# Fused attention and two MLPs on one Trainium2 core: batch 7 and the tails are projected together, by seven half-size products

## The chip, the cores and the metric

The kernel runs on one core of a Trainium2 chip. The metric is device time in microseconds (us) of one execution, from the inputs in the chip's memory to the output there. Engines are named as in the profile: PE (TensorE, matmul), PEld (its weight loads), DVE (VectorE), ACT (ScalarE), POOL (GpSimd), SP (the queue from which nearly all transfers are issued).

## What is computed

```python
def _attn_ref(q, k, v, p):            # q, k, v: (8, 8, 576, 64), p: (8, 8, 32, 64)
    p_packed = sm_attn(p, k, v)       # 32 packed rows per head attend to 576 rows
    out = sm_attn(q, p_packed, p_packed)

def _moe_ref(x, w_in, w_out):         # x: (4608, 512), w_in: (512, 2048), w_out: (2048, 512)
    h = x @ w_in
    g = h * (1.0 / (1.0 + np.exp(-h)))
    return g @ w_out

def _moe2_ref(x, w_in, w_out):        # same shapes
    h = x @ w_in
    g = h * np.clip(h + 3.0, 0.0, 6.0) / 6.0
    return g @ w_out
```

The output is `_moe2(_moe(attention))` over 8 x 576 = 4608 rows.

## The kernel before

A product in single precision is made of three TensorE products of rounded halves: a value is split into a high part (an ACT cast) and a low part (a DVE subtraction), and high x high, high x low and low x high are summed. One such TensorE product has 512 columns and is called a matmul below.

**First phase.** The 4608 rows are worked on as 9 blocks of 512: block j = 0 to 7 holds the first 512 rows of batch j, block 8 the 8 x 64 rows left over, the tails. `block(j)` runs over the 16 chunks f of the hidden dimension. `hidden(j, f)` makes the hidden chunk: 6 matmuls in blocks 0 to 7 (weights `fused`, which `fuse` has made from the packed values and w_in of the first MLP, four chunks at a time; operand `a2`, the attention weights) and 12 in the tails (weights `win`, operand `xh`, `xl`). Then ACT applies Silu in place in the PSUM bank (L891), `split_g` makes the high part on ACT (L898) and the low part on DVE (L899), and two chunks later `projects` multiplies them by w_out: 12 matmuls (L906 to L908) into four accumulators. So PE alternates between hidden chunks and projections. At a block's end ACT and DVE copy the accumulators out, with a write of stride 4 that sorts the rows (L974), and SP stores them to `x1d`.

Beside this stream the attention of batch j + 1 runs, as steps that `attention` lists with a place in the block and waits in units of PE time, and that `Plan` places between matmuls. Its q, k and v come through a ring of 6 tiles called `nat`: the next tile is asked for when one has been used, and SP's transfer waits until DVE has transposed what lay in the buffer. The four v tiles (L348) are used by the packed product (L490, L493). The hidden banks and the attention's banks come from the same four PSUM banks `ps_h`; `fuse` takes two of them.

Half of w_out (even f) stays in the tiles `wr`; odd f is loaded again for each block (`next_out`, L234) into three tiles `wo`.

**Preparation.** The second MLP needs its weights as seven sums of blocks each, so that a product of 2 x 2 blocks takes seven products instead of eight. Class `Prep` makes these from block 1 on, in 32 units, one after the other: load, two ACT steps (L157, L163), two DVE steps, a POOL sum (L297), four DVE sums (L300 to L303), two ACT casts (L305, L306), two POOL subtractions (L308, L309) and three stores. A call of `nxt` between the matmuls runs one step; 9 steps make a unit.

**Second phase.** Class `Second` takes the 4608 rows as five pairs of operands. `Second.project` is its w_out part: 28 steps (7 products x 4 pairs of chunks, order `ORDER_P`) of 12 matmuls, with `sums` (DVE), `split` (ACT cast, DVE subtraction of 128 x 1024) three steps ahead, and weights `ws` by `load_w`.

Of the kernel before, what the change touches and what calls it, by code (L numbers as in the profile page):

```python
# [9 lines left out]
I32 = mybir.dt.int32  # L10
# [8 lines left out]
def tile_pack_attention_two_mlps(ctx: ExitStack, tc, q, k, v, p, w_in1, w_out1, w_in2, w_out2, out):  # L19
# [205 lines left out]
    want_out = [(j, f) for j in range(1, NBLK) for f in range(1, NF, 2)]  # L225
    projected = [-1, -1]

    def next_out():

        now, projected[1] = projected[1], -1 if kept else projected[0]  # L230
        while want_out and now >= NF - 2 and (want_out[0][0] * NF + want_out[0][1]) // 2 <= (now + 1) // 2 - 1 + WO:
            j, f = want_out.pop(0)
            t = half_w(f)
            nc.sync.dma_start(out=f32(t), in_=w1o[f].rearrange("n p f -> p n f"))  # L234
            have_out[j, f] = t
# [4 lines left out]
    w2 = {kind: [dram.tile([S7, P, DM], F32, name=f"w2{kind}{f}", tag=f"w2{kind}{f}") for f in range(HF)] for kind in ("in", "out")}  # L240

    class Prep:


        def __init__(self, pool, w_in, w_out_):
            self.pool = pool
            self.src = {"in": lambda f: win_src(w_in, f), "out": lambda f: wout_src(w_out_, f)}
            self.units = [(kind, f, h) for kind in ("in", "out") for f in range(HF) for h in range(2)]
# [25 lines left out]
        def all(self):  # L274
            self.load(0)
            for _ in range(6):
                yield
            for u, (kind, f, h) in enumerate(self.units):
                key = "p", u
                c = self.pool.tile([P, 8, P], F32, tag="c8", name="c8")  # L280
                hi = self.pool.tile([P, S7, P], F32, tag="hi7", name="hi7", bufs=2)
                conv_begin(key, self.room)
                yield
                yield
                conv_bits(key)
# [12 lines left out]
                yield

                nc.vector.tensor_add(out=c[:, 4], in0=c[:, 2], in1=c[:, 3])  # L300
                nc.vector.tensor_sub(out=c[:, 6], in0=c[:, 0], in1=c[:, 2])
                nc.vector.tensor_sub(out=c[:, 5], in0=c[:, 4], in1=c[:, 0])
                nc.vector.tensor_sub(out=c[:, 7], in0=c[:, 1], in1=c[:, 5])  # L303
                yield
                nc.scalar.copy(out=hi[:, 0:2].bitcast(F32R), in_=c[:, 0:2])  # L305
                nc.scalar.copy(out=hi[:, 2:7].bitcast(F32R), in_=c[:, 3:8])  # L306
                yield
                nc.gpsimd.tensor_sub(out=c[:, 0:2].bitcast(F32R), in0=c[:, 0:2], in1=hi[:, 0:2])  # L308
                nc.gpsimd.tensor_sub(out=c[:, 3:8].bitcast(F32R), in0=c[:, 3:8], in1=hi[:, 2:7])  # L309
                yield  # L310
                yield
                to = w2[kind][f].rearrange("s p f -> p s f")
                nc.sync.dma_start(out=to[:, :, h * P:(h + 1) * P], in_=hi)
                nc.sync.dma_start(out=to[:, 0:2, (2 + h) * P:(3 + h) * P], in_=c[:, 0:2])
                nc.sync.dma_start(out=to[:, 2:7, (2 + h) * P:(3 + h) * P], in_=c[:, 3:8])
# [486 lines left out]
    def attention(b):  # L802
# [18 lines left out]
        add("s", 0.17, 6, lambda: step_s(b), ("kp", 7), (last, 7), bank=9, count=3)  # L821
# [827 lines left out]
```

## Time and profile before

| | us |
|---|---|
| median of 3 runs | 1473.22 (1472.13 to 1473.37) |
| profiled execution, its own time | 1473.38 |
| its span, first to last instruction | 1471.6 |
| PE busy in the span | 1446.9 (98%) |
| DVE, ACT, POOL busy | 1007.9, 725.5, 179.9 |
| moved by transfers | 316.58 MB, 215 GB/s over the span |

Blocks 2 to 6 take some 79 us each, from about 218 to 616 us of the span. Block 7 is the stretch from 616 to 685 us, the tails follow until 774 us, and the rest is the second phase. A busy PE means only that matmuls follow each other; how fast they follow is read from the start times.

### The profile page before, as it was taken

The page shows a single profiled execution, that of the slowest core. Times are in us where ns is not written, and L with a number is a line of the kernel's source. Part 1 is how long each engine was busy: PE and PEld are TensorE (multiplying, and loading weights), DVE is VectorE, ACT ScalarE, POOL GpSimd, SP SyncE. Part 2 cuts the span into 40 slices and gives each one's busy share as a digit, 9 for nine tenths or more (in the row PEclk, how much of TensorE's full clock was granted, in tenths as well). Part 3 has the DMA queues.
Part 4 walks back from the last instruction along what each step waited for, and adds up shares of the span by engine and source line. Part 5 has one row for each costly group of instructions (what it writes and reads, how often), then busy time and mean ns, then how long its engine had stood idle before and what let it go on. Part 6 is the DMA issues. An engine that isn't in the chain of part 4 may idle for free.

```text
span 1471.6 us, 21942 instructions
## 1 busy us (share of the span) xinstructions
PE 1446.9 (98%) x8002; PEld 1178.6 (80%) x8002; DVE 1007.9 (68%) x1555; ACT 725.5 (49%) x1107; POOL 179.9 (12%) x133
## 2 busy tenths in 40 slices
PE   6999999999999999999999999999999999999998
PEld 4767677777777777778888888888888889999998
DVE  5877465566555565545745779776977687788777
ACT  4885455555555555556633344333434353444443
POOL 1440021111112121232320000000000000000000
PEclk9899999999999999999999999999999999999999
DMA  9874868767675866489945575678567866998887
GB/s 289 256 216 131 227 195 214 181 173 181 175 189 163 182 178 174 129 244 254 261 157 194 192 249 195 200 233 260 193 193 224 253 202 218 296 307 252 274 275 224
DMA packets 391051, 316.58 MB, mean 215 GB/s; under 512 B 185120, under 2 KB 288032, under 8 KB 390432
## 3 DMA queue, kind: packets, MB, share of 16 engines
q1 hardware_dynamic: 389048, 314.72, 72.6%
q8 instruction: 64, 1.05, 0.3%
q10 hardware_dynamic: 1896, 0.46, 0.2%
q14 instruction: 43, 0.35, 0.1%
HBM read 257.43 MB, written 57.67 MB: 214 GB/s over the span
## 4 chain that ended last, share of the span: by engine, by line
PE 91%; ACT 4%; DVE 3%; DMA 1%; issue 1%; POOL 0%; SPq 0%; ACTq 0%; POOLq 0%; DVEq 0%
PE acc L906 8%; PE acc L908 8%; PE acc L907 8%; PE b L1172 8%; PE b L1174 8%; PE b L1173 8%; PE b L1267 8%; PE b L1270 8%; PE b L1269 8%; PE hps L879 5%; PE hps L881 5%; PE hps L880 5%; PE abank L426 3%; DMA nat<-in_v_dram 1%; PE abank L490 1%
## 5 line engine op out<-in xcount | busy, mean ns | idle before, releaser
L899 DVE TENSOR_TENSOR gl<-hps,gh 128x512 fp32r<-128x512 f32 x144 | 99.2, 689 | 192.2 <-ACT gh L898 191.8
L1172 PE MATMUL b<-xc,ws 128*128 128x512 f32 (+1 forms) x560 | 205.9, 368 | 0.7 <-ACT x L974 0.7
L1269 PE MATMUL b<-ro,ws 128*128 128x512 f32 (+2 forms) x564 | 206.4, 366 | 0.0
L1270 PE MATMUL b<-ro,ws 128*128 128x512 f32 (+2 forms) x564 | 206.4, 366 | 0.0
L1174 PE MATMUL b<-xc,ws 128*128 128x512 f32 (+1 forms) x560 | 205.8, 367 | 0.0
L1173 PE MATMUL b<-xc,ws 128*128 128x512 f32 (+1 forms) x560 | 205.7, 367 | 0.0
L1215 DVE TENSOR_TENSOR ro<-g,ro 128x1024 fp32r<-128x1024 f32 (+1 forms) x140 | 161.3, 1157 | 42.2 <-ACT ro L1210 41.8
L1210 ACT CAST ro<-g 128x1024 fp32r<-128x1024 f32 (+1 forms) x140 | 131.8, 966 | 94.2 <-DVE g L1203 34.5
L891 ACT ACTIVATE hps<-hps 128x512 f32<-128x512 f32 x144 | 83.9, 583 | 149.9 <-PE hps L881 149.5
L1267 PE MATMUL b<-ro,ws 128*128 128x512 f32 (+2 forms) x564 | 139.0, 367 | 0.3
L906 PE MATMUL acc<-gh,wr 128*128 128x512 f32 x288 | 115.9, 403 | 2.3 <-ACT gh L898 2.3
L1172 PEld LDWEIGHTS b<-xc,ws 128*128 128x128 f32 x560 | 105.2, 188 | 14.2 <-ACT x L974 1.1
L1269 PEld LDWEIGHTS b<-ro,ws 128*128 128x128 f32 x564 | 105.9, 188 | 13.2
L1270 PEld LDWEIGHTS b<-ro,ws 128*128 128x128 f32 x564 | 106.0, 188 | 13.0
L1174 PEld LDWEIGHTS b<-xc,ws 128*128 128x128 f32 x560 | 105.2, 188 | 13.1
L1173 PEld LDWEIGHTS b<-xc,ws 128*128 128x128 f32 x560 | 105.2, 188 | 13.1
L1267 PEld LDWEIGHTS b<-ro,ws 128*128 128x128 f32 x564 | 102.9, 188 | 15.0 <-DVE ro L1215 2.2
L906 PE MATMUL acc<-gh,wo 128*128 128x512 f32 x288 | 113.8, 395 | 0.0
L907 PE MATMUL acc<-gl,wr 128*128 128x512 f32 x288 | 113.4, 394 | 0.2 <-DVE gl L899 0.2
L908 PE MATMUL acc<-gh,wr 128*128 128x512 f32 x288 | 113.3, 393 | 0.0
L908 PE MATMUL acc<-gh,wo 128*128 128x512 f32 x288 | 112.3, 390 | 0.0
L907 PE MATMUL acc<-gl,wo 128*128 128x512 f32 x288 | 112.3, 390 | 0.0
(176 smaller groups left out, 2634.5 us busy)
## 6 DMA issues: line engine op xcount, KB each, us to landing
ws<-w2in SPq DMA_DIRECT2D x280, 256.0 KB
ws<-w2out SPq DMA_DIRECT2D x280, 256.0 KB
wo<-w1o SPq DMA_DIRECT2D x64, 512.0 KB
x1d<-x SPq DMA_DIRECT2D x18, 512.0 KB
raw<-in_moe_w_in_dram SPq DMA_DIRECT2D x16, 512.0 KB
raw<-in_moe_w_out_dram SPq DMA_DIRECT2D x16, 512.0 KB
praw<-in_moe_w_in_dram SPq DMA_DIRECT2D x32, 256.0 KB
praw<-in_moe_w_out_dram SPq DMA_DIRECT2D x32, 256.0 KB
```

The source lines that it names most:

```text
L899: nc.vector.tensor_sub(out=gl, in0=g, in1=f32(gh))
L906: mm(acc[e], lhsT=w[:, 0, s], rhs=gh, start=first, stop=False)
L907: mm(acc[e], lhsT=w[:, 0, s], rhs=gl, start=False, stop=False)
L908: mm(acc[e], lhsT=w[:, 1, s], rhs=gh, start=False, stop=last)
L1172: mm(ps, lhsT=wh, rhs=xs[k][:, 0, c], start=first, stop=False, skip_group_check=True)
L1173: mm(ps, lhsT=wh, rhs=xs[k][:, 1, c], start=False, stop=False, skip_group_check=True)
L1174: mm(ps, lhsT=wl, rhs=xs[k][:, 0, c], start=False, stop=last, skip_group_check=True)
L1210: nc.scalar.copy(out=t[:, 0], in_=v)
L1215: nc.vector.tensor_sub(out=t[:, 1], in0=self.operand(s), in1=f32(t[:, 0]))
L1267: mm(to, lhsT=wh, rhs=x, start=False, stop=last, skip_group_check=True)
L1269: mm(to, lhsT=wh, rhs=x, start=first, stop=False, skip_group_check=True)
L1270: mm(to, lhsT=wl, rhs=x, start=False, stop=False, skip_group_check=True)
```

## The change

Three things are changed.

1. **Batch 7 and the tails as one pair.** Their hidden chunks are computed first, all 16 of batch 7 and then all 16 of the tails. Silu is no longer written in place: ACT writes it from the bank to SBUF tiles `gated`, for batch 7 with the stride of 4 that the block's end had before. Then the new `project_first` multiplies both by w_out as seven products of half size, 28 steps of 12 matmuls, in the way of `Second.project`, and takes over that function's early work for the second phase (`x_steps(0)`).
2. **Preparation.** For this, eight more units ("one") make the seven sums of the first w_out, with 1 KB rows, from the `wr`, `wo` and new `stay` tiles. Units overlap: a unit starts every 10 steps and lasts up to 33. The 40 units run through blocks 1 to 6, batch 7 and 13 of the 16 chunks of the tails; `nxt` runs 1.15 to 1.35 steps per call in 46 calls per block (before: one step in 32 of these calls).
3. **Waits and reloads.** Four of the eight odd w_out chunks stay in SBUF (`STAY`), so four are loaded again per block. Some waits of the attention steps from batch 2 on are shorter or longer by a few units, and all of them from block 1 on are scaled by 1.10.

```diff
-    want_out = [(j, f) for j in range(1, NBLK) for f in range(1, NF, 2)]
+    STAY, SWAP = ((1, 9, 3, 11), (5, 13, 7, 15)), 3
+    stay = {}
+    want_out = [(j, f) for j in range(1, B - 1) for f in range(1, NF, 2)]
...
+    PERIOD, OFFSETS, ONES, ROWS = 10, (3, 13, 16, 17, 18, 21, 23, 25, 29, 31), (0, 6, 4, 12, 8, 13, 29, 28), (9, 33, 20)
...
+                stages = zip(OFFSETS, (self.load, self.begin_unit, self.bits, self.add, self.sums, self.high, self.low, *self.stores(u)))
+                if self.units[u][0] == "one":
+                    stages = zip((*ROWS, *OFFSETS[3:9]), (*self.rows_one(u), self.add_one, self.sums_one, self.high_one, self.low_one, *self.stores_one(u)))
+                for off, fn in stages:
+                    todo.setdefault(PERIOD * u + off, []).append((-off, lambda fn=fn, u=u: fn(u)))
...
+        def add_one(self, u):
+            c = self.c[u] = self.pool.tile([P, 4, 2 * P], F32, tag="c8", name="c1", bufs=2)
+            a, b = (f32(t) for t in self.halves(u))
+            cut = slice(0, 2 * P), slice(2 * P, 4 * P)
+            nc.gpsimd.tensor_add(out=c[:, 1:3], in0=a[:, 0].rearrange("p (r f) -> p r f", r=2), in1=a[:, 1].rearrange("p (r f) -> p r f", r=2))
+            nc.gpsimd.tensor_add(out=c[:, 3], in0=b[:, 0, cut[0]], in1=b[:, 1, cut[0]])
+            nc.gpsimd.tensor_add(out=c[:, 0], in0=b[:, 0, cut[1]], in1=b[:, 1, cut[1]])
...
+        def high_one(self, u):
+            hi = self.hi[u] = self.pool.tile([P, 4, 2 * P], F32, tag="hi7", name="hi1", bufs=2)
+            nc.scalar.copy(out=hi.bitcast(F32R), in_=self.c[u])
+
+        def low_one(self, u):
+            nc.gpsimd.tensor_sub(out=self.c[u].bitcast(F32R), in0=self.c[u], in1=self.hi[u])
...
+        if j >= B - 1:
+            to, src = gated[(f // HF, j - B + 1), f % HF // 2][:, f % 2], ps
+            if j < B:
+                to, src = to.rearrange("p (t i) -> p i t", i=NI), src.rearrange("p (i t) -> p i t", i=NI)
+            nc.scalar.activation(out=to, in_=src, func=AF.Silu)
+            return None
         nc.scalar.activation(out=ps, in_=ps, func=AF.Silu)
...
-            plan.give(11)
+            plan.give(11 if j == 0 else 10)
...
+        def project_first(self):
...
+            for s in range(FD * S7):
+                k, fd = ORDER_P[s // FD], s % FD
+                w, ro = self.weights(), self.ro.pop(s)
+                acc = {1: X, 2: X, 6: Y, 7: Y, 4: Y, 5: Z, 3: Z}[k]
...
+                for lo in range(2):
+                    for f in range(2):
+                        for i in range(2):
+                            wh, wl = (w[:, f, a + i * P:a + (i + 1) * P] for a in (0, 2 * P))
+                            first, last = k in (1, 6, 5) and fd == f == 0, k in (2, 4, 3) and fd == FD - 1 and f == 1
+                            if lo:
+                                mm(acc[i], lhsT=wh, rhs=ro[:, 1, f], start=False, stop=last, skip_group_check=True)
+                            else:
+                                mm(acc[i], lhsT=wh, rhs=ro[:, 0, f], start=first, stop=False, skip_group_check=True)
+                                mm(acc[i], lhsT=wl, rhs=ro[:, 0, f], start=False, stop=False, skip_group_check=True)
+                self.load_w()
...
+                self.sums(s + RO)
+                self.split(s + RO - 1)
+                if s < 2 * FD or s // FD % 2 == 0:
+                    next(prep, None)
...
+    PACE, PACE_LAST, ROOM_AT, X_AT, XS_AT, WIN_AT = (1.25, 1.25, 1.25, 1.35, 1.25, 1.15), (0.9, 0.85), 13, 1, 6, (5, 12, 15)
...
+    for f in range(NF):
...
+        hidden(B - 1, f, nothing, last_work)
+        if f == 2:
+            left()
+        if f % GF == 1 and f // GF + 1 < NG:
+            fuse(B - 1, f // GF + 1)
+        if f == X_AT:
+            load_x()
+        if f in WIN_AT:
+            for g in range(2):
+                win_load(WIN_AT.index(f) * 2 + g)
+        if 0 <= f - XS_AT < KC:
+            split_x(f - XS_AT)
+        if f >= NF - 3:
+            win_split(f - NF + 3)
+    first_right.close()
+    mlp2 = Second()
...
+        hidden(B, f, nothing, last_work if f < ROOM_AT else lambda f, full: None)
...
+    mlp2.project_first()
```

PE, in batch 7, right behind the eight L426 or L488 products that make the second group of hidden weights (the numbers tell tiles apart: `hps` is a hidden bank). Before, a hidden chunk (L879 to L881) is followed by a projection (L906 to L908):

```order
L879 MATMUL hps_6351<-a2h_6113,fused_6154 128x512
L880 MATMUL hps_6351<-a2l_6132,fused_6154 128x512
L881 MATMUL hps_6351<-a2h_6113,fused_6155 128x512
L879 MATMUL hps_6351<-a2h_6223,fused_6157 128x512
L880 MATMUL hps_6351<-a2l_6225,fused_6157 128x512
L881 MATMUL hps_6351<-a2h_6223,fused_6158 128x512
L906 MATMUL acc0_6257<-gh_6289,wo_6198 128x512
L907 MATMUL acc0_6257<-gl_6290,wo_6198 128x512
L908 MATMUL acc0_6257<-gh_6289,wo_6198 128x512
L906 MATMUL acc1_6258<-gh_6289,wo_6198 128x512
L907 MATMUL acc1_6258<-gl_6290,wo_6198 128x512
L908 MATMUL acc1_6258<-gh_6289,wo_6198 128x512
```

The same place now:

```order
L941 MATMUL hps_6394<-a2h_6204,fused_6253 128x512
L942 MATMUL hps_6394<-a2l_6216,fused_6253 128x512
L943 MATMUL hps_6394<-a2h_6204,fused_6254 128x512
L941 MATMUL hps_6394<-a2h_6311,fused_6256 128x512
L942 MATMUL hps_6394<-a2l_6313,fused_6256 128x512
L943 MATMUL hps_6394<-a2h_6311,fused_6257 128x512
L941 MATMUL hps_6409<-a2h_6204,fused_6253 128x512
L942 MATMUL hps_6409<-a2l_6216,fused_6253 128x512
L943 MATMUL hps_6409<-a2h_6204,fused_6254 128x512
L941 MATMUL hps_6409<-a2h_6311,fused_6256 128x512
L942 MATMUL hps_6409<-a2l_6313,fused_6256 128x512
L943 MATMUL hps_6409<-a2h_6311,fused_6257 128x512
```

The projections have moved behind all hidden chunks, so a hidden chunk follows the last one after 6 matmuls instead of 18.

ACT, in the same part of batch 7 (`c8`, `hi7`, `pr`, `praw` are preparation's tiles, `abank` the bank of the hidden weights). Before, a Silu in the bank and a high part per chunk:

```order
L891 ACTIVATE hps_6383<-hps_6383 128x512
L898 CAST gh_6391<-hps_6383 128x512
L157 ACTIVATE pr_6406<-praw_6323 128x512
L163 ACTIVATE praw_6323<-praw_6323 128x512
L891 ACTIVATE hps_6417<-hps_6417 128x512
L898 CAST gh_6427<-hps_6417 128x512
L891 ACTIVATE hps_6451<-hps_6451 128x512
L898 CAST gh_6459<-hps_6451 128x512
L305 CAST hi7_6405<-c8_6404 128x256
L306 CAST hi7_6405<-c8_6404 128x640
L620 CAST fused_6478<-abank_6468 128x512
L620 CAST fused_6481<-abank_6469 128x512
```

Now the Silu writes a gated tile `g` with a stride (4x128), and splits of the tails' operand (`xx`) stand between:

```order
L960 ACTIVATE g04_6421<-hps_6422 128x4x128
L157 ACTIVATE pr_6436<-praw_6306 128x512
L163 ACTIVATE praw_6306<-praw_6306 128x512
L960 ACTIVATE g04_6421<-hps_6430 128x4x128
L682 CAST fused_6456<-abank_6446 128x512
L682 CAST fused_6459<-abank_6447 128x512
L960 ACTIVATE g06_6470<-hps_6471 128x4x128
L1057 CAST xx0_6385<-xx0_6385 128x512
L960 ACTIVATE g06_6470<-hps_6484 128x4x128
L1057 CAST xx1_6387<-xx1_6387 128x512
L960 ACTIVATE g08_6500<-hps_6501 128x4x128
L1057 CAST xx2_6389<-xx2_6389 128x512
```

The high parts are gone from here; since a chunk now takes a third of the matmuls, what is left stands closer together in PE's time.

SP, in block 2, around the loads of the four v tiles (`nat<-in_v_dram`) that the packed product of the next batch needs. Before:

```order
L348 DMA nat_2360<-in_v_dram 128x2x256
L333 DMA pn_2381<-in_p_dram 128x1x64 x2
L339 DMA kt_2384<-in_k_dram 64x8x64
L348 DMA nat_2416<-in_v_dram 128x2x256
L348 DMA nat_2481<-in_v_dram 128x2x256
L234 DMA wo_2497<-w1o7_122 128x2x512
L348 DMA nat_2505<-in_v_dram 128x2x256
L313 DMA w2in1_128<-hi7_2304 128x7x128
```

The same place now:

```order
L410 DMA nat_2347<-in_v_dram 128x2x256
L395 DMA pn_2372<-in_p_dram 128x1x64 x2
L401 DMA kt_2375<-in_k_dram 64x8x64
L334 DMA w2one4_131<-hi1_2317 128x4x256
L410 DMA nat_2406<-in_v_dram 128x2x256
L334 DMA w2one4_131<-c1_2291 128x4x256
L329 DMA w2one2_129<-wr2_705 256x1x256
L410 DMA nat_2472<-in_v_dram 128x2x256
L243 DMA wo_2491<-w1o7_122 128x2x512
L410 DMA nat_2498<-in_v_dram 128x2x256
```

Two stores of 0.5 MB (L334) and one of 0.25 MB (L329) of a "one" unit have come in ahead of the last v tile.

## Rows read from the trace of the kernel before

**Rows 1.** The page, parts 1 and 2: an engine's busy time; PE's granted clock
```profile
PE 1446.9 (98%) x8002; PEld 1178.6 (80%) x8002; DVE 1007.9 (68%) x1555; ACT 725.5 (49%) x1107; POOL 179.9 (12%) x133
...
PEclk9899999999999999999999999999999999999999
```

**Rows 2.** Waits of PE: who waited <- for whom: us, times, longest
```profile
PE abank L490 <- DMA nat<-in_v_dram: 1.8, 1, 1.8
...
PE b L1172 <- ACT x L974: 0.7, 1, 0.7
```

**Rows 3.** Windows: us, busy (instructions) per engine, clock, DMA share, GB/s
```profile
218.00:616.00 398.00, 397.10 (x2529) 293.79 (x2528) 235.25 (x459) 216.49 (x360) 67.44 (x57) 1.00 0.67 175
616.00:685.00 69.00, 69.00 (x337) 54.38 (x336) 30.78 (x61) 40.04 (x71) 21.69 (x18) 1.00 0.84 230
```

**Rows 4.** Timeline of PE in block 7: start us, us, engine, line, operation
```profile
642.98 0.39 PE L879 MATMUL hps<-a2h,fused 128*128 128x512 f32 x1
...
647.06 0.39 PE L879 MATMUL hps<-a2h,fused 128*128 128x512 f32 x1
...
657.04 0.39 PE L908 MATMUL acc<-gh,wr 128*128 128x512 f32 x1
...
658.37 0.50 PE L906 MATMUL acc<-gh,wr 128*128 128x512 f32 x1
```

**Rows 5.** Groups of ACT in block 7: line, operation, count | busy us, mean ns
```profile
L891 ACT ACTIVATE hps<-hps 128x512 f32<-128x512 f32 x16 | 9.3, 582 | 20.5 <-PE hps L881 20.5
L306 ACT CAST hi<-c 128x640 fp32r<-128x640 f32 x6 | 4.4, 729 | 4.1 <-DVE c L303 4.1
L157 ACT ACTIVATE pr<-praw 128x512 f32<-128x512 f32 x6 | 4.1, 677 | 0.0
...
L620 ACT CAST fused<-abank 128x512 fp32r<-128x512 f32 x6 | 3.2, 591 | 1.6 <-PE abank L426 1.6
L305 ACT CAST hi<-c 128x256 fp32r<-128x256 f32 x6 | 2.5, 409 | 0.0
...
L974 ACT COPY x<-acc 128x512 f32<-128x512 f32 x2 | 2.1, 1060 | 3.0 <-PE acc L908 3.0
L222 ACT CAST win<-win 128x512 fp32r<-128x512 f32 x3 | 1.7, 617 | 0.0
```

**Rows 6.** Timeline of ACT in the tails: two starts, and the last copy, without stride
```profile
689.94 0.59 ACT L898 CAST gh<-hps 128x512 fp32r<-128x512 f32 x1
...
692.04 0.58 ACT L891 ACTIVATE hps<-hps 128x512 f32<-128x512 f32 x1
...
773.64 0.58 ACT L974 COPY x<-acc 128x512 f32<-128x512 f32 x1 [0.77 <-PE acc L908]
```

**Rows 7.** Timeline of PE in block 1, around the packed product
```profile
167.32 0.31 PE L490 MATMUL abank<-nat,T 128*32 128x64 f32 x6
169.48 0.63 PE L490 MATMUL abank<-nat,T 128*32 128x64 f32 x26 [1.84 <-DMA nat<-in_v_dram]
...
171.49 0.80 PE L906 MATMUL acc<-gh,wr 128*128 128x512 f32 x1
...
174.10 0.39 PE L879 MATMUL hps<-a2h,fused 128*128 128x512 f32 x1
```

**Rows 8.** The same product on PE in block 3
```profile
330.22 0.65 PE L490 MATMUL abank<-nat,T 128*32 128x64 f32 x32
...
331.88 0.50 PE L906 MATMUL acc<-gh,wr 128*128 128x512 f32 x1
```

**Rows 9.** Window of 10 us in block 2, before its packed product
```profile
235.00:245.00 10.00, 9.93 (x64) 7.26 (x48) 5.28 (x11) 6.30 (x11) 2.26 (x2) 1.00 1.00 280
```

**Rows 10.** Timeline in block 4: a POOL sum of preparation and a DVE step of attention
```profile
352.32 1.57 POOL L309 TENSOR_TENSOR c<-c,hi 128x640 fp32r<-128x640 f32 x1
...
352.73 1.85 DVE L531 TENSOR_TENSOR soft<-soft,s2m 128x640 f32<-128x640 f32 x1
```

**Rows 11.** All of that DVE line: count, min/median/max ns, first to last start
```profile
L531 DVE TENSOR_TENSOR soft<-soft,s2m x16: 691/824/1850, 25.0 to 589.8; 128x512 f32<-128x512 f32 x8, 128x640 f32<-128x640 f32 x8
```

More of the change, by code (lines that the diff above doesn't have):

```diff
@@ L247, in __init__ @@
             self.src = {"in": lambda f: win_src(w_in, f), "out": lambda f: wout_src(w_out_, f)}
-            self.units = [(kind, f, h) for kind in ("in", "out") for f in range(HF) for h in range(2)]
+            rest = [(kind, f, h) for kind in ("in", "out") for f in range(HF) for h in range(2)]
+            ones = dict(zip(ONES, (0, 2, 4, 6, 1, 3, 5, 7)))
+            self.units = [("one", ones[u], 0) if u in ones else rest.pop(0) for u in range(5 * HF)]
+            self.c, self.hi = {}, {}
             self.steps = self.all()
@@ new lines, in all, with halves @@
+            for n in range(max(todo) + 1):
+                for _, fn in sorted(todo.get(n, []), key=lambda x: x[0]):
+                    fn()
+                yield
+        def halves(self, u):
+            f = self.units[u][1]
+            return [made["out", f + n] if f % 2 == 0 else stay[f + n] for n in (0, HF)]
+        def add_one(self, u):
[5 more added lines that the diff above has]
+            nc.gpsimd.tensor_add(out=c[:, 0], in0=b[:, 0, cut[1]], in1=b[:, 1, cut[1]])
@@ new lines, in begin_unit, with bits, add @@
+        def begin_unit(self, u):
+            conv_begin(("p", u), self.room)
+        def bits(self, u):
+            conv_bits(("p", u))
+        def add(self, u):
+            kind, f, h = self.units[u]
+            x, r = raws.pop(("p", u))
+            c = self.c[u] = self.pool.tile([P, 8, P], F32, tag="c8", name="c8", bufs=2)
+            a = c[:, 0:4].bitcast(I32)
+            if kind == "in":
+                a = a.rearrange("p n f -> p (n f)")
+            else:
+                x, r = (t.rearrange("p (b r f) -> p b r f", b=8, r=2) for t in (x, r))
+                a = a.rearrange("p (r n) (b f) -> p (n b) r f", n=2, b=4)
+            nc.gpsimd.tensor_add(out=a, in0=x, in1=r)
@@ L820, in attention @@
             last = f"k{c}"
-        add("s", 0.17, 6, lambda: step_s(b), ("kp", 7), (last, 7), bank=9, count=3)
+        add("s", 0.17, 6, lambda: step_s(b), ("kp", (7 if first else 5)), (last, (7 if first else 5)), bank=(9 if first else 10), count=3)
         steps[-1][4].append((("ut", b - 1), 0))
@@ L1025, in all_chunks @@
         def all_chunks(self):
-            chunks = []
+            chunks = [[w2["one"][2 * fd + i][ROW[k]] for i in range(2)] for k in ORDER_P for fd in range(FD)]
             for n in range(NPAIR):
@@ L1088, in x_steps @@
                 yield
-        def begin_step(self):
-            if next(self.begin, "end") == "end" and self.loaded < WS:
-                self.load_w()
         def bank(self):
@@ L1607, in tile_pack_attention_two_mlps, with last_work @@
             feed.end()
-        if j == B:
-            prep.end()
-        plan.slow = 1
-    for _ in mlp2.begin:
-        pass
+        plan.slow = 1.10
+    def last_work(f, full):
+        share[0] += PACE_LAST[part_[0]]
+        while share[0] >= 1:
+            share[0] -= 1
+            prep.step()
+    part_ = [0]
+    nothing = lambda: None
+    for f in range(NF):
+        if f % 2 == 0:
+            if f < NF // 2:
+                gated[(0, 0), f // 2] = wts.tile([P, 2, T], F32, tag=f"wr{f}", name=f"g0{f}")
+            else:
+                if f % 4 == 0:
+                    two = wts.tile([P, 2, 2, T], F32, tag=f"wr{f}", name=f"g0{f}")
+                gated[(1, 0), f % HF // 2] = two[:, f % 4 // 2]
+        hidden(B - 1, f, nothing, last_work)
[14 more added lines that the diff above has]
+    mlp2 = Second()
+    part_[0] = 1
+    for f in range(NF):
+        if f % 2 == 0:
+            tag, n = [("wo", WO), ("g", LAG), ("x1", 2)][(f // 2 > 2) + (f // 2 > 5)]
+            gated[(f // HF, 1), f % HF // 2] = gp.tile([P, 2, T], F32, tag=tag, name=f"g1{f}", bufs=n)
+        if f == ROOM_AT:
+            prep.end()
+            prep_room.close()
+            mlp2.enter()
+        hidden(B, f, nothing, last_work if f < ROOM_AT else lambda f, full: None)
+        if f % 2 and f < HF:
+            mlp2.t1(f // 2)
+        if f >= NF - 2:
+            mlp2.split(f - NF + 2)
+    mlp2.project_first()
     first_left.close()
```

196 lines of the change are left out of this document (114 added, 82 removed).

## The prediction

> **What bounds the kernel now.** I read the page's busy shares first, then the waits of PE, then the start times of PE, and last what ACT, DVE and POOL do in the stretches that the change touches. PE is busy for 1446.9 of 1471.6 us at a granted clock that stands at full level from the third slice on [rows 1]. Of its waits two matter here, 1.8 us for a v tile in block 1 and 0.7 us at the change of phase [rows 2]; in blocks 2 to 7 it waits for next to nothing (397.10 busy of 398.00, and 69.00 of 69.00) [rows 3]. The chunk that starts at 642.98 and the next one, at 647.06, are 18 matmuls apart: 4.08 us, so one matmul per 0.2267 us [rows 4]. (A row's own 0.39 us is its modelled length, not its pace.) PE is the bound, so the time moves by the matmuls taken away, less each new wait of PE. ACT and DVE have room on the average (235 and 294 of 398 us) [rows 3], and what counts is whether they have it at each place.
>
> **The change part by part.** The counts of instructions, read from the order of both kernels, differ on PE by 48 matmuls of 128x512 and nothing else: w_out of batch 7 and the tails took 2 x 16 x 12 = 384, now 28 x 12 = 336. At 0.2267 us [rows 4] that is **-10.88 us**. It lies on PE's own path whole, since the granted clock is full there [rows 1].
>
> The Trainium skill, "TensorE: Matmul & The Clock Gate", section "Back-to-back issue gap", gives about 131 ns as the sustained spacing of 512-column matmuls; by it the 48 would be worth 6.3 us and the median would come out 4.6 us above my forecast. The trace says otherwise for this kernel's operands, 226.7 ns, and that is what I use.
>
> *Batch 7's hidden chunks.* Before, ACT had 18 matmuls of PE time per chunk, now it has 6: 96 x 0.2267 plus three makings of hidden weights. Such a making costs PE about 1.2 us (658.37 - 657.04, less part of the slot that is there anyway) [rows 4]; together 25.4 us. In that time ACT has to do 16 Silus, and these now write with a stride. No row shows a strided Silu. The bounds are the Silu in place, 582 ns [rows 5], and the strided copy at a block's end, 1060 ns [rows 5], where the copy without a stride takes 0.58 [rows 6]. The write has the same stride as that copy, so I take 1.06: 17.0 us. Beside them stand, by the order, 6 casts of hidden weights (0.591), 3 pairs of high parts (0.409 + 0.729), 2 pairs of L157 and L163 (0.677 for the one, the other taken alike), 4 casts of the tails' operand and 2 of its weights (0.617, one shape) [rows 5]: 3.5 + 3.4 + 2.7 + 3.7 = 13.3 us. One strided copy of block 6, 1.06, falls in too. ACT has 31.4 us of durations for 25.4 us of PE. But ACT's neighbours overlap: from 689.94 to 692.04 four operations with durations of 2.35 us start within 2.10 us [rows 5, 6]. By that factor, 0.89, ACT needs 28.1 us, an overshoot of 2.7 us; without it, 6.0. PE is held only when no hidden bank is free. Of four banks the making of weights takes two, and of the other two one is being filled, so ACT may lag by one chunk, 6 x 0.2267 = 1.4 us. Left is **+1.3 us** (bounds: 0, with the Silu at 0.58 or a lag of two chunks, and 6.0). The tails' chunks have 12 matmuls each and Silus without stride, so ACT catches up there and nothing else is held.
>
> *The projection.* Its 28 steps have the form of the second phase's `project`, which sums, splits and loads in the same way, three steps ahead, and is not among PE's waits [rows 2]; so they cost their matmuls and nothing more. If that cover is gone, a step of 2.7 us (12 x 0.2267) is the most that one late operand costs. The 0.7 us wait at the change of phase [rows 2] stood behind the last strided copies; the new early work `x_steps(0)` runs inside the projection as before inside the tails, so I leave it as it is (bounds: 0.7 gained, 1.2 lost for one step's first operand).
>
> *Preparation and transfers.* The eight new units store three rows of 0.25 MB and two tiles of 0.5 MB each, some 14 MB; 32 reloads of 0.5 MB fall away, so the sum is about even. Per block it is not: about 7.2 units instead of 4 run in blocks 1 to 6, some 1.4 MB each, less four reloads: 2.4 MB more in 79 us, which lifts 175 GB/s [rows 3] to about 205. Block 7 ran at 230 GB/s and a share of 0.84 with no wait of PE [rows 3]. SP's queue is the delicate place: two stores and a row of a "one" unit now stand ahead of v tiles that the packed product needs, and SP serves in order. Already now the 10 us before that product in block 2 run at a share of 1.00 and 280 GB/s [rows 9]. What a late v tile costs is seen in block 1: from the product's first matmul at 167.32 to the next projection at 171.49 it takes 4.17 us, of which 1.84 is the wait, against 330.22 to 331.88, 1.66 us, in block 3; and the six matmuls after it take 2.61 us instead of 6 x 0.2267 = 1.36 [rows 7, 8]. That is 2.5 + 1.2 = **3.7 us per late tile**. The bytes from the block's x1d store to the last v tile, added up along SP's order, are 4.3 MB in block 1 before (late), 2.8 to 4.2 in blocks 2 to 6 (not late), and 3.7 to 4.6 now, with the packed product three matmuls later than before. So the blocks come closer to the edge, but few beyond it. I take **+1.0 us**: a short wait in one or two blocks (bounds: -3.7, if block 1 is on time, and five more events, 18).
>
> *DVE and POOL.* The preparation's POOL sums and subtractions run about twice as often per block. One DVE step took 1.85 us while a POOL subtraction of 1.57 us ran beside it [rows 10]; the same line has a median of 0.824 us and a minimum of 0.691 [rows 11]. So a collision can cost DVE 1.0 us. The attention's steps are placed with room between them (7 to 15 matmuls, 1.6 to 3.4 us), and these are scaled up by 1.10. I take **+0.5 us** (bounds: 0, and 1.0 us in each of six blocks).
>
> Sum: 1473.38 - 10.88 + 1.3 + 1.0 + 0.5 = 1465.3 us. That is against the profiled execution; the median lies 0.16 us lower, so 1465.1.
>
> **The rivals.**
>
> *Nothing new waits.* Banks absorb ACT's lag and every v tile is in time: 1473.2 - 10.9 = 1462.3; with block 1's wait gone too, 1458.6. For it: 69.00 of 69.00 busy at 0.84 [rows 3]. Against: one window at 1.00 [rows 9].
>
> *ACT sets batch 7 in full.* The durations add up as they stand and the makings of weights leave no slack: 1462.3 + 6.0 + 1.5 = 1469.8. For it: the strided copy's 1060 ns [rows 5]. Against: the overlap in [rows 6].
>
> *DVE stands behind POOL in every block.* A collision of 1.0 us falls on the softmax's chain in each of six blocks and the room does not cover it: 1462.3 + 1.3 + 1.0 + 6.2 = 1470.8, about no change. The trace has one such row and fifteen others that are mostly short [rows 11]. The Trainium skill, "GPSIMD Engine Reference", section "1. Specifications", says that POOL shares its SBUF interfaces with VectorE and contends with DVE instructions that have two SBUF inputs; it speaks against more work on POOL, and the stretched row with two such inputs agrees with it [rows 10].
>
> *Late v tiles, slower than before.* The stores on SP's queue push the last v tile of several blocks behind its product, 3.7 us each. After the 10.9 gained and the 1.8 of the other terms some 9 us are left: two and a half events eat the gain, and from four on it is slower: 1462.3 + 1.8 + 14.8 = 1478.9. For it: block 1's event with 4.3 MB ahead [rows 7]. Against: block 3 on time [rows 8] with 4.2 MB ahead.
>
> **How the numbers follow.** Forecast 1465.1, chance 0.56. Nothing new waits: 0.18. ACT in full: 0.08. DVE behind POOL: 0.07. Late v tiles: 0.11. A measurement of this kernel tells about 0.2% from no change: 1470.3 and 1476.2 are the bounds. Faster takes the forecast, the clean case and half of ACT in full, 0.78; same takes the rest of that, DVE behind POOL and a little of the late tiles, 0.12; slower is the rest of these, 0.10. The range runs from just under the clean case, 1461.5, to just over DVE behind POOL, 1472; outside lie the late tiles (0.11) and the clean case with block 1's wait gone (about 0.05).
>
> **What would show it.** PE should have 48 matmuls less, in the stretch of the projection. In batch 7, waits of PE at a hidden bank for ACT's Silu (L960), 1 to 2 us together, with Silus of about 1060 ns; Silus near 600 ns and no wait would mean the clean case. In blocks 1 to 6, waits of the packed product (L552) for v tiles (L410): one short one or two is my sum, one per block the slow rival. DVE steps of the attention above 1.5 us beside POOL in each block, with PE waiting for DVE, would be the third rival. The forecast is wrong if PE's wait in the projection for `ro` or the weights is more than 2 us, or if the granted clock falls in a stretch behind such a wait, of which no row here tells the price except the six slow matmuls in block 1 [rows 7].

## The result

The changed kernel takes 1460.34 us (median of 4 runs, 1459.04 to 1460.55), the kernel before 1473.3 us beside it: a ratio of 0.9915, 95% interval 0.9903 to 0.9927. That is 13.0 us less, where 8.1 us were forecast, and the time lies 1.2 us below the range.

The page of the changed kernel, parts 1 and 2, against [rows 1]:

```profile
PE 1435.6 (98%) x7954; PEld 1167.9 (80%) x7954; DVE 1055.5 (72%) x1603; ACT 748.1 (51%) x1113; POOL 224.4 (15%) x166
...
PEclk8899999999999999999999999999999999999999
```

PE has 11.3 us less to do, in 48 matmuls less; DVE, ACT and POOL have 48, 23 and 45 us more. The waits of PE, against [rows 2] (who waited <- for whom: us, times, longest):

```profile
PE abank L537 <- DVE gg L970: 1.8, 2, 0.9
...
PE b L1396 <- DVE ro L1344: 0.4, 1, 0.4
```

The wait for a v tile is gone, and so is the one at the change of phase. A wait on DVE has come, once in block 0 (there it stood before too) and once in block 4. The 0.4 us on `ro` is not in the new projection but near the end of the second phase:

```profile
1414.35 0.96 PE L1396 MATMUL b<-ro,ws 128*128 128x384 f32 x4 [0.39 <-DVE ro L1344]
```

Where the time went is read by stage: the start of each block's first hidden product in PE's timeline, in the profiled executions. The last column is the whole span.

| us | to block 1 | block 1 | blocks 2 to 6 | batch 7 to second phase | second phase | span |
|---|---|---|---|---|---|---|
| before | 138.4 | 82.6 | 396.4 | 156.9 | 697.3 | 1471.6 |
| after | 138.5 | 78.9 | 397.0 | 146.1 | 698.2 | 1458.7 |
| difference | +0.1 | -3.6 | +0.6 | -10.8 | +0.9 | -12.9 |

So 10.8 us come from the projection, as was worked out, and 3.6 us from block 1, where the forecast had no gain. The same two places in the trace of the changed kernel. PE in block 1, against [rows 7] (start us, us, operation):

```profile
167.10 1.09 PE L488 MATMUL abank<-wi,ppT 64*32 64x512 f32 x16
168.12 0.65 PE L552 MATMUL abank<-nat,T 128*32 128x64 f32 x32
168.70 0.32 PE L555 MATMUL abank<-vt,a1t 64*32 64x64 f32 x8
```

All 32 matmuls of the packed product run in 0.65 us, as in block 3 before [rows 8], where in block 1 they stopped after six. And the windows of batch 7's hidden chunks, the tails' and the projection, against [rows 3] (us, busy per engine, clock, DMA share, GB/s):

```profile
614.40:640.20 25.80, 25.78 (x145) 18.23 (x144) 13.48 (x30) 24.40 (x35) 9.57 (x7) 1.00 0.84 227
640.20:685.80 45.60, 45.60 (x201) 37.47 (x201) 30.27 (x46) 29.74 (x54) 21.34 (x14) 1.00 0.89 249
685.80:760.50 74.70, 74.70 (x330) 61.50 (x329) 62.38 (x57) 36.03 (x39) 2.41 (x1) 1.00 0.72 239
```

In batch 7 ACT is busy for 24.40 of 25.80 us, close to its limit, and PE for 25.78. The full clock is granted in all three. (The projection begins at 684.0, so its first eight products fall in the second row.)

A second reading was needed for blocks 1 to 6. Each has 288 matmuls and seven bursts of the attention, and a block in which nothing waits takes 78.83 us in every kernel here. Six such blocks are 473.0 us; before took 478.9, after 475.9. What a kernel takes over 473.0 is its loss to waits there.

### The profile page after: what moved, and what is told of

Its sections match the earlier page's. It is cut to its first block, busy times and chain, and to the rows that moved or that the text cites. A ratio compares the mean times of both kernels' runs of the same rounds, so it can differ in the third digit from the quotient of the medians.

```text
span 1458.7 us, 22051 instructions
## 1 busy us (share of the span) xinstructions
PE 1435.6 (98%) x7954; PEld 1167.9 (80%) x7954; DVE 1055.5 (72%) x1603; ACT 748.1 (51%) x1113; POOL 224.4 (15%) x166
## 4 chain that ended last, share of the span: by engine, by line
PE 93%; ACT 3%; DVE 1%; DMA 1%; issue 1%; SPq 0%; POOL 0%; ACTq 0%; POOLq 0%; DVEq 0%
PE b L1301 8%; PE b L1302 8%; PE b L1303 8%; PE b L1396 8%; PE b L1398 8%; PE b L1399 8%; PE acc L977 7%; PE acc L979 6%; PE acc L978 6%; PE hps L941 5%; PE hps L943 5%; PE hps L942 5%; PE abank L488 4%; PE pX L1121 1%; PE pX L1122 1%; PE pX L1119 1%
## 5 line engine op out<-in xcount | busy, mean ns | idle before, releaser
L1344 DVE TENSOR_TENSOR ro<-g,ro 128x1024 fp32r<-128x1024 f32 (+1 forms) x168 | 196.7, 1176 | 59.8 <-ACT ro L1339 54.6
L1339 ACT CAST ro<-g 128x1024 fp32r<-128x1024 f32 (+1 forms) x168 | 160.5, 980 | 112.3 <-DVE g L1332 41.5
L970 DVE TENSOR_TENSOR gg<-hps,gg 128x512 fp32r<-128x512 f32 x112 | 77.1, 689 | 114.9 <-ACT gg L969 113.0
L962 ACT ACTIVATE hps<-hps 128x512 f32<-128x512 f32 x112 | 65.4, 584 | 106.4 <-PE hps L943 103.0
L1380 POOL TENSOR_TENSOR ov<-ov,o 128x1024 f32<-128x1024 f32 (+1 forms) x5 | 10.9, 2185 | 693.2 <-ACT ov L1368 693.2
L941 PE MATMUL hps<-a2h,fused 128*128 128x512 f32 x256 | 102.8, 402 | 1.6 <-ACT fused L682 1.6
L943 PE MATMUL hps<-a2h,fused 128*128 128x512 f32 x256 | 100.1, 391 | 0.0
L942 PE MATMUL hps<-a2l,fused 128*128 128x512 f32 x256 | 99.8, 390 | 0.0
L977 PE MATMUL acc<-gg,wr 128*128 128x512 f32 x224 | 90.3, 403 | 1.9 <-ACT gg L969 1.9
L977 PE MATMUL acc<-gg,wo 128*128 128x512 f32 x224 | 88.8, 397 | 0.0
```

Of the source, the lines that this page charges most:

```text
L941: mm(ps, lhsT=wh, rhs=rh, start=c == 0, stop=False)
L942: mm(ps, lhsT=wh, rhs=rl, start=False, stop=False)
L943: mm(ps, lhsT=wl, rhs=rh, start=False, stop=c == len(parts) - 1)
L977: mm(acc[e], lhsT=w[:, 0, s], rhs=gh, start=first, stop=False)
L1339: nc.scalar.copy(out=t[:, 0], in_=v)
L1344: nc.vector.tensor_sub(out=t[:, 1], in0=self.operand(s), in1=f32(t[:, 0]))
```

## The experiments

The expectations name blocks and stages as above. Where the text says "by the medians", it compares with 1471.97 us, the median of 19 executions of the kernel before beside four of these kernels (1470.31 to 1474.7); by that one the change is worth 11.6 us. Measured times without a ratio are of one execution. All stages in us:

| | to block 1 | block 1 | blocks 2 to 6 | batch 7 to second phase | span |
|---|---|---|---|---|---|
| a_eight | 138.5 | 78.9 | 396.3 | 157.0 | 1468.1 |
| a_plain | 139.9 | 78.9 | 396.9 | 145.5 | 1459.0 |
| a_silu2 | 138.7 | 78.9 | 396.7 | 154.1 | 1466.5 |
| b_waits | 138.4 | 80.1 | 395.3 | 156.9 | 1468.3 |
| b_late | 138.1 | 78.9 | 395.9 | 157.3 | 1467.7 |
| a_oldwaits | 138.2 | 80.1 | 400.3 | 146.1 | 1462.9 |
| before_again | 138.5 | 82.8 | 395.5 | 156.9 | 1471.3 |
| before_third | 137.9 | 80.8 | 396.3 | 156.9 | 1469.4 |
| a_pool2 | 137.9 | 79.9 | 403.2 | 151.7 | 1470.7 |
| a_sums | 138.4 | 79.7 | 396.9 | 146.4 | 1459.5 |
| a_s19 | 138.0 | 79.1 | 396.8 | 146.4 | 1458.4 |
| a_pace | 138.1 | 78.9 | 397.5 | 146.0 | 1458.2 |

### The saved matmuls

```diff
-                for lo in range(2):
+                for lo in (0, 1, 0, 1) if k == 1 else (0, 1):
```

> The changed kernel with one of the seven products of the projection done twice: 4 steps, 48 matmuls more, the number that the change saves; its sum is counted twice, so the output differs. If the matmuls lie on the path whole, 48 x 0.2267 = 10.9 us more, 1471.2, and then the change without its saving is still 2 us below before. If the projection's operands or weights were the bound of its steps, less than 8 us.

Measured: 1470.58 us (ratio to before 0.9991, 0.9982 to 1.0001). The last stage that it touches grew from 146.09 to 156.97 us, by 10.88: 48 x 0.2267 to the hundredth. So the projection is bound by PE alone, and without its saving the change is worth what blocks 1 to 6 give, some 1.4 us by the medians and 3.5 by the spans.

### ACT in batch 7

```diff
-            if j < B:
-                to, src = to.rearrange("p (t i) -> p i t", i=NI), src.rearrange("p (i t) -> p i t", i=NI)
```

> The changed kernel with batch 7's Silu written without the stride; the sorting of rows is left out, so batch 7's rows come out in another order. The Silu should fall from 1.10 to about 0.6 us, ACT's work in batch 7 by 7 us. By the prediction's term ACT held PE there for 1.3 us, which would come back: 1459.0. By the trace of the change (batch 7 took 25.85 us for 25.4 us of PE work) at most 0.5 us comes back, 1460, so the banks cover ACT's lag.

Measured: 1459.47 us (ratio 0.9913, 0.9898 to 0.9927). Batch 7 to the second phase fell from 146.09 to 145.54, by 0.55 us. The span is no shorter than the change's, since this execution took 1.4 us longer to reach block 1. The Silu without the stride (L958 in this kernel; duration ns min/median/max):

```profile
L958 ACT ACTIVATE g<-hps x32: 585/598/612, 617.2 to 684.9; 128x512 f32<-128x512 f32 x32
```

With the stride, in the changed kernel, first chunk and last chunk of batch 7 on ACT:

```profile
615.96 1.10 ACT L960 ACTIVATE g<-hps 128x512 f32<-128x512 f32 x1 [0.26 <-PE hps L943]
...
642.22 1.09 ACT L960 ACTIVATE g<-hps 128x512 f32<-128x512 f32 x1
```

So the size of the strided Silu was right (1.06 taken, 1.10 measured), and its cost to PE is 0.5 us, not 1.3. ACT's last Silu of batch 7 ends at 643.3; after a product that ends at 640.2, with 0.26 us to start and 1.1 to run, it would end at 641.6. The lag is about 1.8 us, where 2.7 had been worked out. How much lag the banks cover was asked apart:

```diff
-            nc.scalar.activation(out=to, in_=src, func=AF.Silu)
+            for _ in range(2 if j < B and f % 2 else 1):
+                nc.scalar.activation(out=to, in_=src, func=AF.Silu)
```

> The changed kernel with batch 7's Silu done twice in 8 of its 16 chunks (the same values written again): some 8 x 0.97 = 7.8 us more for ACT. In the changed kernel ACT ends batch 7's Silus about 1.8 us later than PE's last product would ask, so the lag becomes 9.6 us. By the prediction (a lag of one chunk, 1.4 us, is covered) PE loses about 8 us: the stretch from batch 7 to the second phase, 146.1 us, goes to 154. If the four banks cover three chunks, 4.1 us, it loses 5 to 6 us: 151 to 152.

Measured: the stretch took 154.1 us, 8.0 more. Batch 7 alone went from 25.85 to 33.16. PE waits there now (waits of PE from 610 to 650 us):

```profile
PE hps L941 <- ACT g L961: 3.5, 3, 1.8
PE hps L941 <- ACT win L222: 0.3, 1, 0.3
PE abank L488 <- ACT g L961: 0.2, 1, 0.2
```

Nearly all that was added to ACT (8.2 us) came out as PE's time. That fits the cover of one chunk that the prediction took, and says that the changed kernel has used it up.

### Block 1's v tile

Two things of the change could have ended the wait: the attention's waits (the packed product comes later) and the order of transfers. First the waits alone, in the kernel before:

```diff
-        add("s", 0.17, 6, lambda: step_s(b), ("kp", 7), (last, 7), bank=9, count=3)
+        add("s", 0.17, 6, lambda: step_s(b), ("kp", (7 if first else 5)), (last, (7 if first else 5)), bank=(9 if first else 10), count=3)
...
-            plan.give(11)
+            plan.give(11 if j == 0 else 10)
...
-        plan.slow = 1
+        plan.slow = 1.10
```

(and the units of the other steps as in the change)

> The kernel before with one part of the change: the attention's waits (their units, the scale of 1.10 from block 1 on, and the room given after a chunk, 10 for 11). Nothing else is moved. Theory A (the later packed product and the earlier v loads end block 1's wait): the 1.8 us wait of the packed product on the v tile is gone and block 1 falls from 82.6 to about 79 us, so the time is about 3.6 us below before, 1469.7. Rival B (the wait went because preparation's transfers stand elsewhere in the queue): the wait stays, within 1 us of before, 1473.

Measured: 1470.44 us (ratio 0.9991, 0.9981 to 1.0). Block 1 is 2.5 us shorter than in the first trace of before and block 2 1.1 us; the wait is shorter but there:

```profile
168.06 0.31 PE L490 MATMUL abank<-nat,T 128*32 128x64 f32 x6
169.19 0.63 PE L490 MATMUL abank<-nat,T 128*32 128x64 f32 x26 [0.82 <-DMA nat<-in_v_dram]
```

Neither theory came out whole. The product came 0.74 us later and the wait fell by 1.0. Then the reverse, the changed kernel with the old waits:

```diff
-            plan.give(11 if j == 0 else 10)
+            plan.give(11)
...
-        plan.slow = 1.10
+        plan.slow = 1
```

(and the units of the attention's steps as before)

> The changed kernel with the attention's waits as before (units, scale 1, room 11). Theory A: block 1's packed product waits for its v tile again, about 3.6 us more, 1464. Rival B: block 1 stays near 79 us; time within 1.5 us of the change, 1459 to 1462.

Measured: 1464.67 us (ratio 0.9949, 0.9934 to 0.9963), 4.3 above the change. But the wait for a v tile came back as no more than 0.2 us of a weight load (who waited for the v loads):

```profile
  PEld abank L552: 0.2, 1
```

Block 1 lost 1.1 us and blocks 2 to 6 lost 3.4 us, mostly to other waits. The rows of over 0.3 us that the changed kernel does not have are on DVE, and make 1.5 of these 4.5 us; the rest is not in the list:

```profile
PE abank L656 <- DVE a2l L632: 0.8, 1, 0.8
PE abank L488 <- DVE gg L970: 0.7, 2, 0.4
```

So theory A got the price and the wrong place, and rival B the v tile. That leaves the rest of the change, preparation and its transfers. Preparation was moved out of the first half of block 1, in the kernel before:

```diff
-            if j:
+            if j and not (j == 1 and f < 8):
...
-                for _ in range(1 + (j == B - 1 and calls[0] % 6 == 0) if j >= B - 1 else full):
+                for _ in range(1 + (j == B - 1 and calls[0] % 3 == 0) if j >= B - 1 else full):
```

> The kernel before with preparation started half a block later (no step of it in the first 8 chunks of block 1; two steps more often in batch 7 and the tails), so that none of its loads or stores stands near block 1's v tiles; the attention's waits are those of before. If preparation's transfers made the v tile late, the 1.8 us wait goes and block 1 falls from 82.6 to 79 to 80 us. If the packed product is simply asked for too early, the wait stays above 1 us and block 1 above 81.5.

Measured: block 1 took 78.93 us, quiet, with the old waits, and the time was 1469.5 beside 1472.47 in one run each. SP's queue in both kernels, first before, then this one (start us, us to issue):

```profile
160.23 0.97 SPq L264 DMA_DIRECT2D praw<-in_moe_w_in_dram  x2
161.30 0.41 SPq L234 DMA_DIRECT2D wo<-w1o  x1
161.82 0.41 SPq L348 DMA_DIRECT2D nat<-in_v_dram  x1
```

```profile
158.99 0.42 SPq L234 DMA_DIRECT2D wo<-w1o  x1
160.80 0.37 SPq L348 DMA_DIRECT2D nat<-in_v_dram  x1
```

Without preparation's two `praw` loads ahead, the last v tile is issued 1.0 us earlier (0.7 us, counted from the block's start) and has 0.5 MB less before it. The edit also takes preparation's steps off DVE, and in both kernels SP waits for DVE to free the v tiles' buffers (5.3 and 6.1 us); this run does not tell the two apart. In the changed kernel the two loads stand there still, but the tile is issued earlier and used later:

```profile
159.39 0.99 SPq L278 DMA_DIRECT2D praw<-in_moe_w_in_dram  x2
160.42 0.47 SPq L243 DMA_DIRECT2D wo<-w1o  x1
161.24 0.37 SPq L410 DMA_DIRECT2D nat<-in_v_dram  x1
```

Issue to use is 168.12 - 161.24 = 6.9 us, against 167.32 - 161.82 = 5.5 before. That alone would not end the wait: before, PE went on only 7.7 us after the issue (169.48 - 161.82). The tile also lands sooner now, 6.4 us after its issue, the longest of this line in the changed kernel (issue to landing, us):

```profile
DMA to landing us min/median/max: 3.4/4.5/6.4
```

So the tile gained 1.4 us from issue to use and some 1.3 us from issue to landing, against a wait of 1.84 us; neither is enough by itself. How short the time to landing can be is seen in block 4 of the changed kernel, where 4.2 us from issue to use bring no wait:

```profile
402.88 0.37 SPq L410 DMA_DIRECT2D nat<-in_v_dram  x1
```

```profile
407.08 0.65 PE L552 MATMUL abank<-nat,T 128*32 128x64 f32 x32
```

The attention's waits alone take about half of block 1's wait away (b_waits), and the rest of the change alone all but 0.2 us of it (a_oldwaits). Why the tile lands sooner is not shown.

The medians of the waits alone show 1.5 us, the traces 3.6. So before was looked at twice more:

> The kernel before once more, unchanged, to see whether block 1's wait is the same in every execution. By the stages of the profiled executions the attention's waits alone are worth 3.6 us (blocks 1 to 6 from 478.9 to 475.4), by the medians 1.5 us. If the wait on the v tile varies from execution to execution, block 1 comes out between 79 and 82.6 us here, and the other blocks as before within 0.3 us each. If it is always there, block 1 is 82.6 again within 0.3 us.

> The same once more. If the wait varies, this execution's block 1 differs from the first two by more than 0.3 us at least once in the three; if it is always there, all three show 82.6 within 0.3 us and a wait of 1.5 to 2 us on the v tile.

Measured: the wait is in all three, 1.8, 2.0 and 1.6 us, but block 1 takes 82.6, 82.8 and 80.8 us. Windows of PE right behind the wait, the granted clock third from the right, first before, then the third execution:

```profile
169.40:171.40 2.00, 1.92 (x74) 1.49 (x74) 0.00 (x0) 0.00 (x0) 0.00 (x0) 0.79 0.99 254
171.40:174.10 2.70, 2.70 (x14) 2.09 (x7) 0.91 (x2) 0.00 (x0) 0.00 (x0) 0.53 0.46 87
```

```profile
168.80:170.50 1.70, 1.70 (x75) 1.33 (x75) 0.10 (x1) 0.00 (x0) 0.00 (x0) 1.00 1.10 301
170.50:174.00 3.50, 3.50 (x16) 2.88 (x17) 0.91 (x2) 1.19 (x3) 0.00 (x0) 1.00 0.51 89
```

Behind the wait of 1.84 us the granted clock is 0.53 for 2.7 us, its lower level, 1.2 GHz (in the second execution 0.50); behind the one of 1.62 us it stays full. That is the rest of the 3.7 us that the prediction put on a late tile. Blocks 1 to 6 of before are 478.9, 478.2 and 477.2; the gain from them is therefore 1.3 to 3.1 us, by execution, and the first trace is at the upper end.

### DVE behind POOL

Block 4 of the changed kernel lost 2.1 us. All engines from 397 to 403 us, the rows that make the chain:

```profile
399.29 1.30 POOL L352 TENSOR_TENSOR c<-pr,praw 128x512 int32<-128x512 int32 x1 [7.92 <-DMA w2in<-c]
...
400.62 0.29 DVE L356 TENSOR_TENSOR c<-c 128x128 f32<-128x128 f32 x1 [2.85 <-POOL c L352]
...
402.16 0.70 DVE L455 STREAM_TRANSPOSE T<-nat 128x512 f32<-128x512 f32 x1
...
402.30 0.41 PE L537 MATMUL abank<-ident,soft 128*64 128x128 f32 x2 [0.88 <-DVE gg L970]
```

POOL waits for a store of the unit two before to leave its tile, DVE's sum waits 2.85 us for POOL, the attention's and the stream's DVE steps stand behind that sum in order, and PE waits for one of them. That is 0.9 of the 2.1 us. Another 1.0 us is lost earlier in the block, in a burst of 16 products that takes 2.10 us, where the same burst in block 3 takes 1.09:

```profile
310.24 1.09 PE L488 MATMUL abank<-T,pT 64*32 64x512 f32 x16
...
389.09 2.10 PE L488 MATMUL abank<-T,pT 64*32 64x512 f32 x16
```

```profile
388.77 0.69 DVE L970 TENSOR_TENSOR gg<-hps,gg 128x512 fp32r<-128x512 f32 x1 [1.71 <-ACT gg L969]
389.38 0.70 DVE L455 STREAM_TRANSPOSE T<-nat 128x512 f32<-128x512 f32 x1
```

There the transpose that PE needs stands on DVE behind a step that waits for ACT, not for POOL. To see whether this is what the units cost, POOL's step was doubled:

```diff
-            nc.gpsimd.tensor_add(out=a, in0=x, in1=r)
+            for _ in range(2):
+                nc.gpsimd.tensor_add(out=a, in0=x, in1=r)
```

> The changed kernel with POOL's sum at the head of each of the 32 old units done twice (the same values written again): 1.3 us more of POOL per unit, some 40 us in all, ahead of DVE's sums that wait for it in order. If DVE behind POOL is what lengthens the attention's bursts on PE, blocks 1 to 6 (475.9 us; six quiet blocks would be 473.0) grow by more than 2 us, with waits of PE on DVE. If the longer waits cover DVE's delay, they stay within 0.7 us.

Measured: blocks 1 to 6 took 483.1 us, 7.2 more, and batch 7 and the tails 5.6 more. Waits of PE from 130 to 620 us:

```profile
PE hps L942 <- DVE gg L971: 2.2, 3, 0.8
PE abank L538 <- DVE gg L971: 1.4, 1, 1.4
PE abank L489 <- DVE T L456: 1.4, 1, 1.4
```

DVE's own busy time did not grow (1055.2 us, 1055.5 in the changed kernel), so its steps were not stretched by the 42 us more of POOL: they came later. PE does pay for POOL, through DVE's order. With the old waits (a_oldwaits) the six blocks took 480.4, 7.4 us over quiet ones, with the new ones 2.9: the longer waits are what pays for the overlapping units. Three tries to take the rest:

```diff
-    PERIOD, OFFSETS, ONES, ROWS = 10, (3, 13, 16, 17, 18, 21, 23, 25, 29, 31), (0, 6, 4, 12, 8, 13, 29, 28), (9, 33, 20)
+    PERIOD, OFFSETS, ONES, ROWS = 10, (3, 13, 16, 17, 19, 21, 23, 25, 27, 28), (0, 6, 4, 12, 8, 13, 29, 28), (9, 33, 20)
```

> The changed kernel with DVE's sums of a unit one step later behind POOL's sum (19 for 18) and the stores two and three steps earlier (27 and 28 for 29 and 31), so that POOL finds its tile free sooner and DVE finds POOL's sum done. If block 4's 0.9 us wait of PE on DVE comes from DVE standing behind POOL, which stands behind a store, it goes: block 4 falls from 80.9 by 1 us or more and the time to about 1459. If something else delays DVE there, block 4 stays.

Measured: 1461.31 us in one run. The wait on DVE in block 4 went and block 5 became quiet, but block 1 lost 0.8 us and block 4 stayed at 81.2, for another wait (waits of PE in the whole span):

```profile
PE abank L552 <- DMA nat<-in_v_dram: 1.4, 1, 1.4
```

That is the late v tile that the prediction had as its slow rival: stores moved forward by two or three steps are enough to bring it, in one block.

```diff
-    PERIOD, OFFSETS, ONES, ROWS = 10, (3, 13, 16, 17, 18, 21, 23, 25, 29, 31), (0, 6, 4, 12, 8, 13, 29, 28), (9, 33, 20)
+    PERIOD, OFFSETS, ONES, ROWS = 10, (3, 13, 16, 17, 19, 21, 23, 25, 29, 31), (0, 6, 4, 12, 8, 13, 29, 28), (9, 33, 20)
```

> The changed kernel with DVE's sums of a unit one step later behind POOL's sum (19 for 18) and the stores where the change has them. If DVE standing behind POOL is what is left over a quiet block (78.83 us) in blocks 2, 4 and 5, these three fall (79.2, 80.9, 79.2 now) by 0.3 us or more each, and no v tile is late, since the queue is not touched: blocks 1 to 6 together 474 or less, from 475.9. If the earlier stores were what quieted blocks 2, 3 and 5 in the run with both, nothing falls.

Measured: 1460.24 us in one run; blocks 1 to 6 together 475.9, as before the edit. Block 5 became quiet (78.83 for 79.17), block 2 stayed and block 4 lost 0.2 more. POOL's wait for the store is still there, and DVE's with it (POOL and DVE in block 4 of this kernel):

```profile
399.10 1.29 POOL L352 TENSOR_TENSOR c<-pr,praw 128x512 int32<-128x512 int32 x1 [8.49 <-DMA w2in<-c]
```

```profile
400.43 0.29 DVE L356 TENSOR_TENSOR c<-c 128x128 f32<-128x128 f32 x1 [3.42 <-POOL c L352]
```

```diff
-    PACE, PACE_LAST, ROOM_AT, X_AT, XS_AT, WIN_AT = (1.25, 1.25, 1.25, 1.35, 1.25, 1.15), (0.9, 0.85), 13, 1, 6, (5, 12, 15)
+    PACE, PACE_LAST, ROOM_AT, X_AT, XS_AT, WIN_AT = (1.25, 1.25, 1.25, 1.25, 1.25, 1.25), (0.9, 0.85), 13, 1, 6, (5, 12, 15)
```

> The changed kernel with the same pace of preparation, 1.25 steps per call, in all of blocks 1 to 6 (for 1.35 in block 4 and 1.15 in block 6). Block 4 holds 2.1 of the 2.9 us that blocks 1 to 6 take over six quiet blocks. If its faster pace brings the units together with the attention there, block 4 falls below 80 us and block 6 stays under 79.5. If the place of the units against the attention's steps decides, the loss only moves to other blocks and the sum stays within 1 us of 475.9.

Measured: 1460.01 us in one run; block 4 fell to 80.3 and block 5 rose to 80.3, the six blocks took 476.4. The loss moved. No version here beats the change by what a measurement can tell. A third buffer for POOL's tile, which might end its wait for the store, wasn't tried.

## Why the prediction was wrong

The working, term by term, against the first traces:

| us | predicted | measured |
|---|---|---|
| 48 matmuls | -10.9 | -10.9 (a_eight) |
| ACT in batch 7 | +1.3 | +0.5 (a_plain) |
| change of phase | 0 | -0.7 |
| the projection's steps, beside their matmuls | 0 | +0.3 |
| v tiles, and the attention's waits in block 1 | +1.0 | -3.6 |
| DVE behind POOL | +0.5 | +0.6 (all of blocks 2 to 6) |
| start and second phase | 0 | +1.0 (0.4 of it the wait for `ro`) |

**The step that failed is the one on v tiles.** It gave the bytes ahead of the last v tile, 3.7 to 4.6 MB, the say over whether it is late, and took "a short wait in one or two blocks", +1.0. By that sum block 1 is worse off now: the same loads as before, 4.3 MB, and a row of 0.25 MB, 4.6 MB together, and yet its tile is in time.

```profile
153.92 0.97 SPq L329 DMA_DIRECT2D w2one<-wr  x1
```

What decides is the time from issue to use against the time from issue to landing: 5.5 against some 7.7 us before in block 1, 6.9 against 6.4 now. The first of the two could have been asked for before the run: the order showed the packed product three matmuls later, which the text mentions, and the wait to be covered was 1.84 us [rows 7]. The end where block 1 is on time stood among the bounds, and with it the case of 1458.6 us, at a chance of about 0.05 and outside the range. Its time and the measured one differ by ACT's 0.5 us, blocks 2 to 6, the projection's 0.3 us and the second phase, less the 0.7 us at the change of phase.

**The change's third part had no term.** The longer and scaled waits were only named as cover for DVE. They are worth 1.5 us by the medians and up to 3.6 by the traces on the kernel before (b_waits), and 4.3 us on the changed one (a_oldwaits).

**DVE behind POOL** came out near its size, 0.6 us in blocks 2 to 6, by luck: it is a balance of waits that went and waits that came (2.2 us over quiet blocks before, 2.8 now), and the mechanism is another. The prediction priced a DVE step that is stretched beside POOL [rows 10]. Such steps are there: the same line now has a maximum of 2.61 us (L593), against 1.85 before [rows 11].

```profile
L593 DVE TENSOR_TENSOR soft<-soft,s2m x16: 691/824/2611, 25.1 to 586.9; 128x512 f32<-128x512 f32 x8, 128x640 f32<-128x640 f32 x8
```

The Trainium skill, "GPSIMD Engine Reference", section "1. Specifications", tells of that contention, and the stretched rows agree with it. But no wait of PE hangs on it here: what reached PE is DVE's order, behind POOL's result and once behind ACT's.

**ACT in batch 7**: the price of the strided Silu and the cover of one chunk were right, the lag was sized 0.9 us too high. **The saving of the projection** came out to the hundredth; its 28 steps cost 0.3 us beside their matmuls, where nothing was forecast. **The change of phase** was left as it is, and its 0.7 us went. (The prediction puts that wait behind strided copies; by [rows 6] the last copy there has no stride.)

**The 48 matmuls by the Trainium skill's spacing.** The 131 ns of "TensorE: Matmul & The Clock Gate", section "Back-to-back issue gap", that the prediction set against the trace would have made them 6.3 us; 10.88 us for 48 is 226.7 ns each.

What stays open: why the tile in block 1 lands sooner; why the second phase and its end take up to 0.9 us more in the profiled executions of kernels with the change (697.4 to 698.2) than in those without it (697.3 to 697.6), where the changed kernel's wait for `ro` is 0.4 us and the stretch behind PE's last product 5.6 us, 4.9 before; and why a wait of about the same length takes the granted clock down in two executions and not in the third.

## What to carry to other kernels

A wait in the trace of before is a term of its own: ask first whether the change ends it, by the time from issue to use against that from issue to landing, before counting what new waits may come. Where units of work on three engines are made to overlap, the engine that serves them in order passes their delays to everything behind it; what pays for that are longer distances in the stream beside it, so the two edits are costed as one. And where a loss of a microsecond sits in one of six like blocks, compare each block with a quiet one before turning a knob: three knobs here only moved it.

## What the runs showed of the hardware

A Silu of 128x512 from PSUM to SBUF took 1.10 us with a write of stride 4 and 0.598 without. A wait of PE of 1.84 or 2.0 us was followed by 2.7 to 3.1 us at a granted clock of 0.53 or 0.50, one of 1.62 us by none; the block lost 3.7 or 3.9 us in the first two cases and 2.0 in the third. A load of 0.25 MB landed 6.4 us after its issue in block 1 of the changed kernel and within 4.2 us in block 4. Nothing else was unexpected.
